# First group of a fused attention and gated-MLP kernel: products on GpSimd, scores one place ahead, no selecting products

## The chip, the cores and the metric

The kernel runs on one core of a Trainium2 chip. The metric is the device time of one execution in microseconds. Lower is better. One execution was also recorded by the hardware profiler; its span, and every instant below, counts from the span's start.

## The reference, cut to what matters

Two batches of 768 tokens with 8 heads of 48 pass a linear attention with a decaying state, then a layer with a squared relu and a sigmoid gate, then a gated layer that mixes tokens.

```python
for t in range(S):                       # attention, per batch and head
    cur = einsum('bhd,bhe->bhde', u * k_t, v_t)
    y[:, :, t] = einsum('bhd,bhde->bhe', r_t, state + cur)
    state = w_t[..., None] * state + einsum('bhd,bhe->bhde', k_t, v_t)
x = y laid out as (B, S, 384)
xk = mu_k * x + (1 - mu_k) * x_prev      # x_prev: one token back
xr = mu_r * x + (1 - mu_r) * x_prev
x = sigmoid(xr @ w_r) * (relu(xk @ w_k)**2 @ w_v)
h = gelu(x @ w_in); u, v = halves of h
v_s = einsum('ts,bsd->btd', w_sg, layernorm(v) * g) + b
out = x + (u * v_s) @ w_out
```

## The kernel before, in words

The tokens are cut into four groups of 384 (three chunks of 128), and the heads into four pairs. A unit is one pair of heads in one group, so units 0 to 3 are the first group and unit 4 opens the second. Inside a chunk the decays are turned into running products, so that the attention becomes products on TensorE (PE). The steps of unit i are these.

- Prep, on VectorE (DVE): a forward scan of the decays (`pf`), three reciprocals, a backward scan (`pr`), then `kp` = k times `pr`, `rp` = r times `pf`, and `ru` = r times k. `pr` has one buffer, `ru` two.
- S: PE transposes `kp` (`kt_ps`, which ScalarE, ACT, copies to `kt`), makes the scores `sc` from `kp` and `rp`, and sums `ru` with a small matrix `hmu` (the "sums"). DVE masks the scores (`am`, two instructions) and scales v by the sums (`vb`).
- K: PE makes each chunk's contribution to the state, `kv`; DVE chains them (`zt`, `zcar`), ACT scales them to the matrices `sblk` (and `scar`, carried to the next group).
- Y: PE applies `am` and `vb` to give `y`. Z: PE adds `sblk` times `rp`; ACT copies `y` out to `yo`, and SyncE (SP) moves its rows by DMA into `xx`, where features lie on partitions, three tiles of 128.

Then the first layer starts: `xkh` mixes a token with the one before it (ACT makes `dx`, DVE adds), one third of the features at a time, here xkh(0) to xkh(2), and PE multiplies it with eight tiles of weights, k0 to k7, three products each. Each weight tile comes by DMA as 64-bit words; ACT converts one part (`top`) and DVE joins the rest to `wk`.

The first group's order on DVE and ACT is the order in which the code is written: a class `in_order` chains these instructions. PE follows its program order everywhere. Of the rest, a scheduler orders by due times that come from a written plan (`TS`, `TE`), and instructions traced later may be placed among those of the chain. So every engine's order is fixed before the run, and an instruction that waits holds back all behind it on its engine. In the head PE also runs idle products (`dummy`).

Before the change the plan of the first group is S, K, Y, Z per unit, with the last two interleaved. GpSimd (POOL) makes only `ru`, and does so while DVE masks. Unit 1's last feature rows and those of units 2 and 3 reach xkh(1) and xkh(2) not by the DMAs but by four selecting products on PE (`sel_run`, line 650), which write them into a bank of PSUM (`sel_bank`).

Of the kernel before, what the change touches and what calls it, by code (L numbers as in the profile page):

```python
# [48 lines left out]
T_GAP = 2.5  # L49
# [14 lines left out]
ST0 = 1.04  # L64
# [6 lines left out]
def emit(tc, tin, nin, vt, consts, ucp, pars, b_sg, w_k, w_v, w_r, w_in, w_sgT, w_out, outT):  # L71
# [54 lines left out]
    u = [unit_plan(i) for i in range(NP)]  # L126
    for i in range(NP - 2):
        plan += list(u[i])
    plan += u[NP - 2][:3] + u[NP - 1][:1] + u[NP - 2][3:] + u[NP - 1][1:]
    plan = [(key, d * ST0) for key, d in plan]  # L130
# [155 lines left out]
    def load64(full, src, dl, lc=L_CV):  # L286
# [9 lines left out]
        if n_ < N_EARLY + B_STG + KF // 2:  # L296
            ld = T_EARLY + n_ * D_EARLY
# [113 lines left out]
    def attn_prep(i):  # L411
# [32 lines left out]
    def rk_make(i, e=V):  # L444
        rks[i] = pa.tile([PR, subs[i // NP][2] * CH], F32, name="ru", tag="ru", bufs=2)
        with at(TS["S", i] - L_PREP + (2 if i == 0 else -4)):
            return e.tensor_tensor(rks[i], urk[i][:, 0], urk[i][:, 1], ALU.mult).ins  # L447

    def attn_sc(i):
        tS, tK, tY = TS["S", i], TS["K", i], TS["Y", i]  # L450
# [17 lines left out]
        am = pa.tile([128, 2, nc_, CH], F32, name="am", tag="am", bufs=B_AM)
# [16 lines left out]
        if i < NP:  # L485
            sums(head["bs"][0][:, 0:2 * nc_])
        self_am(i, am, sc, tY)
        vb = pa.tile([128, nc_, 2, D], F32, name="vb", tag="vb", bufs=2)
        with at(tK - 1.6 if i >= NP else tY - 1.4):
            bh = s["bs"].rearrange("p (c h) -> p c h", h=2)[:, :, :, None].to_broadcast([128, nc_, 2, D])  # L490
            V.tensor_tensor(vb, uv[i].rearrange("p c (h d) -> p c h d", h=2), bh, ALU.mult)
        s["vb"] = vb
# [7 lines left out]
    def self_am(i, am, sc, tY):  # L500
# [75 lines left out]
    def attn_z(i):  # L576
# [58 lines left out]
    def sel_make():  # L635
        t = klpair(F32)
        sel = [t[0:PR, q * 128:q * 128 + 128] for q in range(4)]
        PL.memset(t, 0.0)
        head["sel"] = sel
        for q, rows_, to, fr in ((0, slice(32, D), 0, 32), (0, slice(HP, PR), 16, HP), (1, slice(0, D), 64, 0),  # L640
                                 (1, slice(HP, HP + 16), 112, HP), (2, slice(HP, PR), 0, HP + 16),
                                 (3, slice(0, D), 32, 0), (3, slice(HP, PR), 80, HP)):
            n = min(rows_.stop, PR) - rows_.start if q != 2 else 32
            A.activation(sel[q][rows_, to:to + n], ident[rows_, fr:fr + n], AF.Copy)

    def sel_bank(j):
        return head["bs"][j % 2]

    def sel_run(q):
        PE.matmul(sel_bank(1 + q // 2)[:, 1:1 + G], head["sel"][q], st[1 + (q + 1) // 2]["yo"], start=(q % 2 == 0), stop=(q % 2 == 1))  # L650

    def moe1_prep(s, which, hold=(), mix=None):
# [259 lines left out]
    fns = {"S": attn_sc, "K": attn_kv, "Y": attn_y, "Z": attn_z, "k": moe1_k, "r": moe1_r, "v": moe1_v,  # L912
# [39 lines left out]
    with at(TS["k", 0, 0] - 14):  # L952
        SP.dma_start(par, pars)
# [35 lines left out]
    V.memset(head["bs"][1][:, 0:1], 0.0)
    scans(0)  # L990
    products(0)
    scans(1)
# [161 lines left out]
```

## Time and profile before

| what | value |
|---|---|
| median of three runs | 340.63 us (339.87 to 341.85) |
| the profiled execution's own time | 340.49 us |
| its span | 338.6 us |
| PE busy | 329.6 us, 97% of the span |
| DVE, ACT, POOL busy | 235.9, 186.2 and 37.4 us |
| chain that ended last, PE's share | 84% |

The profiled execution takes 1.89 us more than its span, which lies around the recorded work, and stands 0.14 us under the median. PE's busy time says how long it had an instruction in flight. It counts idle products too, so the head's waits must be read from the order of instructions.

### The profile page before, as it was taken

The numbers are of one execution on the slowest core, as the hardware profiler recorded it, in microseconds if no ns is written. First come the engines' busy times: TensorE is split into PE (matmuls) and PEld (weight loads), VectorE is DVE, ScalarE is ACT, GpSimd is POOL, SyncE is SP. The second block draws the span as 40 slices with busy tenths as digits, with TensorE's granted clock in tenths as the row PEclk, the third lists the DMA queues.
The fourth block names the chain that finished last, engine by engine and source line by source line (L and its number), as shares of the span: only waits on it lengthen the run. The fifth ranks groups of instructions, "written<-read, shape, count | busy, mean of one in ns | idle before, by whom it ended". The sixth has DMA issues, their size and how long they took to land.

```text
span 338.6 us, 5946 instructions
## 1 busy us (share of the span) xinstructions
PE 329.6 (97%) x2139; PEld 286.8 (85%) x2139; DVE 235.9 (70%) x527; ACT 186.2 (55%) x444; POOL 37.4 (11%) x60
## 2 busy tenths in 40 slices
PE   7999999999999999999999999999999999999993
PEld 3785666666788899888899999989999999999993
DVE  5988987699799873996459551696889833645531
ACT  3557976568868633976339973866353216211100
POOL 3221203010110100111022531000000000000000
PEclk9999999999999999999999999999999999999998
DMA  8887955753616430011025314613230010100022
GB/s 211 211 256 256 293 190 145 195 138 99 183 58 187 115 89 9 18 38 36 19 64 180 102 57 141 171 42 82 62 81 22 1 70 2 46 25 0 0 75 77
DMA packets 24006, 34.27 MB, mean 101 GB/s; under 512 B 3568, under 2 KB 18288, under 8 KB 23968
## 3 DMA queue, kind: packets, MB, share of 16 engines
q1 hardware_dynamic: 21824, 31.39, 31.9%
q10 hardware_dynamic: 2144, 2.41, 2.9%
q8 instruction: 19, 0.31, 0.4%
q14 instruction: 19, 0.16, 0.2%
HBM read 29.07 MB, written 2.36 MB: 93 GB/s over the span
## 4 chain that ended last, share of the span: by engine, by line
PE 84%; DVE 5%; ACT 4%; DMA 3%; issue 1%; SPq 0%; ACTq 0%; DVEq 0%
PE mm L631 40%; PE mn L631 28%; PE y L570 3%; PE sc L477 3%; PE y L584 2%; DMA cst<-consts 2%; PE kv L526 1%; PE ab L473 1%; PE y L573 1%; PE kt_ps L455 1%; DMA stg<-w_in 1%; PE mm L650 1%; ACT wh L317 1%; DVE pf L425 1%; PE mm L460 1%
## 5 line engine op out<-in xcount | busy, mean ns | idle before, releaser
L619 ACT ACTIVATE gah<-gt 128x384 fp32r<-128x384 f32 x16 | 8.4, 526 | 43.4 <-DVE gt L810 43.4
L447 POOL TENSOR_TENSOR ru<-urk 112x384 f32<-112x384 f32 x15 | 17.6, 1173 | 113.3 <-DVE ru L480 81.7
L552 ACT ACTIVATE sblk<-zt,pf 48x48 f32<-48x48 f32 x62 | 20.5, 331 | 16.8 <-DVE zt L536 10.5
L716 DVE TENSOR_TENSOR kl<-kr,kh 128x384 fp32r<-128x384 f32 x24 | 15.6, 649 | 9.6 <-ACT kr L715 9.6
L631 PE MATMUL mm<-kh,wh 128*128 128x384 f32 x64 | 22.2, 347 | 0.0
L631 PE MATMUL mm<-kh,wvl 128*128 128x384 f32 x64 | 21.6, 337 | 0.0
L631 PE MATMUL mm<-kl,wh 128*128 128x384 f32 x64 | 21.5, 336 | 0.0
L631 PE MATMUL mm<-xkh,wh 128*128 128x384 f32 x57 | 20.3, 356 | 0.0
L631 PE MATMUL mn<-wsh,vl 128*128 128x384 f32 x60 | 20.0, 334 | 0.0
L631 PE MATMUL mn<-wsh,vh 128*128 128x384 f32 x60 | 20.0, 334 | 0.0
L631 PE MATMUL mn<-wsl,vh 128*128 128x384 f32 x60 | 20.0, 334 | 0.0
L665 ACT ACTIVATE dx<-xx,par 128x384 f32<-128x384 f32 x22 | 12.9, 609 | 11.6 <-DMA xx<-yo 11.5
L631 PE MATMUL mm<-xkl,wh 128*128 128x384 f32 x57 | 19.2, 338 | 0.0
L631 PE MATMUL mm<-xkh,wkl 128*128 128x384 f32 x57 | 19.2, 337 | 0.0
L506 DVE TENSOR_TENSOR am<-sc,cst 128x384 f32<-128x384 f32 x32 | 16.3, 547 | 1.9 <-PE sc L477 1.9
L477 PEld LDWEIGHTS sc<-rp,kp 48*128 48x128 f32 x192 | 12.0, 187 | 6.2 <-issue 5.6
L425 DVE TENSOR_TENSOR_SCAN pf<-uw,d1f 112x387 f32<-112x387 f32 x16 | 15.3, 957 | 2.5 <-DMA uw<-tin 2.5
L631 PE MATMUL mm<-xkh,wk 128*128 128x384 f32 x48 | 17.0, 497 | 0.0
L701 ACT ACTIVATE kr<-mm 128x384 f32<-128x384 f32 x27 | 12.9, 478 | 7.5 <-PE mm L631 7.3
L318 POOL TENSOR_TENSOR w2l<-wf,w2h 128x384 fp32r<-128x384 f32 x12 | 12.9, 1092 | 35.7 <-ACT w2h L317 35.7
L631 PE MATMUL mm<-kh,wv 128*128 128x384 f32 x48 | 16.3, 490 | 0.0
L430 DVE TENSOR_TENSOR_SCAN pr<-uw,d1r 112x387 f32<-112x387 f32 x16 | 15.8, 984 | 0.4
(218 smaller groups left out, 969.0 us busy)
## 6 DMA issues: line engine op xcount, KB each, us to landing
urk<-tin SPq DMA_DIRECT2D x26, 144.0 KB, 3.0
wh<-w_k SPq DMA_DIRECT2D x8, 384.0 KB, 4.9
stg<-w_in SPq DMA_DIRECT2D x8, 384.0 KB, 3.6
wq<-tin SPq DMA_DIRECT2D x16, 168.0 KB, 2.5
wsf<-w_sgT SPq DMA_DIRECT2D x12, 192.0 KB, 3.8
outT<-ot SPq DMA_DIRECT2D x12, 192.0 KB, 1.9
uv<-nin ACTq DMA_DIRECT2D x14, 144.0 KB, 3.5
uw<-tin SPq DMA_DIRECT2D x26, 72.8 KB, 2.9
```

The lines of the kernel that those rows point to most:

```text
L318: e.tensor_tensor(lo, full, hi.bitcast(F32), ALU.subtract)
L425: V.tensor_tensor_scan(pf[:, 0:n1], w[:, 0:n1], d1f[:, 0:n1], 1.0, ALU.mult, ALU.max)
L430: V.tensor_tensor_scan(pr[:, 1:wl][:, ::-1], w[:, 1:wl][:, ::-1], dr[:, 1:wl][:, ::-1], 0.0, ALU.mult, ALU.add)
L447: return e.tensor_tensor(rks[i], urk[i][:, 0], urk[i][:, 1], ALU.mult).ins
L477: PE.matmul(sc[h][:, c], s["kp"][hs, c], s["rp"][hs, c], start=True, stop=True)
L506: s["am"] = V.tensor_tensor(am[:, h], sc[h], mask, ALU.mult).ins
L552: s["sa"] = A.activation(sb[hs, hs], o[hs], AF.Copy, scale=s["pe"][c][hs]).ins
L570: PE.matmul(y3[hs, c], uv[i][:, c, h * D:PW if h else HP], s["at"][:, h, c], start=(c == 0), stop=False, skip_group_check=True)
L631: PE.matmul(ps, l, r, start=(first and k == 0), stop=(last and k == len(prods) - 1))
L665: ins = [A.activation(d, xj[:, 1 + t0:1 + t1], AF.Copy, scale=mu[:, j:j + 1]).ins]
L701: m1[s, "ev", f] = A.activation(kr, ps, AF.Relu).ins
L716: V.tensor_tensor(kl, kr, kh.bitcast(F32), ALU.subtract)
```

## The change

GpSimd makes `kp`, `rp` and `ru` of units 1 to 3, and `ru` of unit 0; DVE keeps unit 0's `kp` and `rp`. `hmu` is one DVE instruction instead of four on ACT. Prep runs two units ahead. S is split into T (transposes), S (scores) and U (sums), and PE takes T(i), Y(i-1), S(i), Z(i-1), U(i), K(i). The selecting products and their matrices go; xkh(1) and xkh(2) read `xx`, as xkh(0) did. Tiles k0 to k2 are done side by side, all on xkh(0), then on xkh(1), then on xkh(2). Six k weight tiles are loaded early. There are fewer idle products (two after the first scores, one before T(1)).

```diff
@@ plan
-    plan += u[NP - 2][:3] + u[NP - 1][:1] + u[NP - 2][3:] + u[NP - 1][1:]
+    for i in range(NP):
+        n = subs[0][2]
+        plan += [(("T", i), 0.13 * n)]
+        if i:
+            plan += [(("Y", i - 1), Y_D * n)]
+        plan += [(("S", i), 0.3 * n)]
+        if i:
+            plan += [(("Z", i - 1), 0.18 * n)]
+        plan += [(("U", i), 0.25 * n), (("K", i), 0.17 * n)]
@@ load64
-            ld = T_EARLY + n_ * D_EARLY
+            ld = TS["T", 1] + 0.1 * n_ if n_ < N_HEAD else TS["k", 0, 0] + (n_ - N_HEAD) * D_EARLY
@@ attn_prep
+        if 1 <= i < NP:
+            in_turn(PL.tensor_tensor, kp, k3, pr3[:, :, 0:CH], ALU.mult)
+            in_turn(PL.tensor_tensor, rp, r3, pf3[:, :, 0:CH], ALU.mult)
+            rk_make(i)
+        else:
...
+            if i == 0:
+                rk_make(0, last)
+                V.tensor_tensor(hmu, hm[:, None, :].to_broadcast([PR, NP, 2]),
+                                u_sb[:, :, None].to_broadcast([PR, NP, 2]), ALU.mult)
@@ moe1_prep
-            xj = sel_bank(j) if s == 0 and mix is not None and j else x[:, j]
+            xj = x[:, j]
@@ moe1_k
-        mm(ps, [(part(wt["k", f], slice(None), j), part(m1[s, 0], slice(None), j)) for j in range(KM)])
+        first = 3 if s == 0 and split_ops[0] else 1
+        if 0 < f < first:
+            return
+        fs = range(f, f + first if f == 0 else f + 1)
+        ps = [mm_tile()[:, 0:nt] for _ in fs]
+        for j in range(KM):
+            for p, f in zip(ps, fs):
+                mm(p, [(part(wt["k", f], slice(None), j), part(m1[s, 0], slice(None), j))], j == 0, j == KM - 1)
@@ the loop over the plan
+        if kd == "K" and g < NP - 2:
+            scans(g + 2)
+            products(g + 2)
+        if kd == "T" and 0 < g or key == ("K", NP - 1):
+            for f in st[g - 1 if kd == "T" else g].pop("soon"):
+                f()
+        if key == ("T", NP - 1):
+            conv_moe1(0, 2)
+        if key == ("Z", NP - 2):
+            mix = []
+            moe1_prep(0, 0, mix=mix)
+            mix[0]()
```

GpSimd's program in the first group, of before: four products, one per unit from unit 1 on (the last row but one belongs to unit 4), with the mixing parameters' complement `par1` among them.

```order
L447 TENSOR_TENSOR ru_207<-urk1_109 112x384
L447 TENSOR_TENSOR ru_286<-urk2_110 112x384
L447 TENSOR_TENSOR ru_365<-urk0_108 112x384
L954 TENSOR_SCALAR par1_76<-par_75 128x6
L447 TENSOR_TENSOR ru_426<-urk1_109 112x384
L611 COPY xx1_78<-xx0_77 128x3
```

The same place of the change:

```order
L463 TENSOR_TENSOR ru_159<-urk0_108 112x384
L463 TENSOR_TENSOR kp_169<-urk1_109,pr_167 112x384
L463 TENSOR_TENSOR rp_168<-urk1_109,pf_166 112x384
L463 TENSOR_TENSOR ru_175<-urk1_109 112x384
L984 TENSOR_SCALAR par1_76<-par_75 128x6
L463 TENSOR_TENSOR kp_221<-urk2_110,pr_219 112x384
L463 TENSOR_TENSOR rp_220<-urk2_110,pf_218 112x384
L463 TENSOR_TENSOR ru_227<-urk2_110 112x384
L463 TENSOR_TENSOR kp_299<-urk0_108,pr_297 112x384
L463 TENSOR_TENSOR rp_298<-urk0_108,pf_296 112x384
L463 TENSOR_TENSOR ru_305<-urk0_108 112x384
L470 TENSOR_TENSOR ru_411<-urk1_109 112x384
```

Ten products stand where three stood, in turn, `kp`, `rp`, `ru` of each unit.

DVE from the last unit's `sblk` to xkh(2), of before (`xkh` from `mm` reads a bank that a selecting product wrote; the `wk` here is k1; `pf` and `pr` are unit 4's).

```order
L550 TENSOR_SCALAR sblk11_89<-zt_445,pf_313 48x48 x2
L667 SCALAR_TENSOR_TENSOR xkh_392<-xx0_77,par1_76,dx_454 128x384
L667 SCALAR_TENSOR_TENSOR xkh_392<-mm_136,par1_76,dx_457 128x384
L425 SCALAR_TENSOR_TENSOR pf_487<-uw1_106,d1f_72 112x387
L427 RECIPROCAL d1r_90<-pf_487 112x3
L313 SCALAR_TENSOR_TENSOR wk_494<-wh_495,top1_129 128x384
L667 SCALAR_TENSOR_TENSOR xkh_392<-mm_135,par1_76,dx_500 128x384
```

The same place of the change (the five `wk` are k2 to k6):

```order
L590 TENSOR_SCALAR sblk11_89<-zt_436,pf_296 48x48 x2
L321 SCALAR_TENSOR_TENSOR wk_471<-wh_472,top0_128 128x384
L686 SCALAR_TENSOR_TENSOR xkh_420<-xx0_77,par1_76,dx_476 128x384
L321 SCALAR_TENSOR_TENSOR wk_479<-wh_480,top1_129 128x384
L433 SCALAR_TENSOR_TENSOR pf_484<-uw1_106,d1f_72 112x387
L321 SCALAR_TENSOR_TENSOR wk_576<-wh_577,top0_128 128x384
L435 RECIPROCAL d1r_90<-pf_484 112x3
L321 SCALAR_TENSOR_TENSOR wk_581<-wh_582,top1_129 128x384
L438 SCALAR_TENSOR_TENSOR pr_485<-uw1_106,d1r_90 112x387
L321 SCALAR_TENSOR_TENSOR wk_586<-wh_587,top0_128 128x384
L686 SCALAR_TENSOR_TENSOR xkh_420<-xx0_77,par1_76,dx_491 128x384
```

Nine instructions now stand between the start of k2's `wk` and xkh(2), with unit 4's two scans among them; xkh(0) has moved ahead of this piece.

ACT in the change, from the last transposes' copy to xkh(2)'s `dx` (`top0` and `top1` alternate through k0 to k6; the DMA issues of v are left out).

```order
L492 ACTIVATE kt_371<-kt_ps_367 128x336
L592 ACTIVATE sblk00_86<-zt_363,pf_218 48x48 x2
L592 ACTIVATE sblk01_87<-zt_363,pf_218 48x48 x2
L319 ACTIVATE top0_128<-wh_378 128x384
L319 ACTIVATE top1_129<-wh_383 128x384
L632 ACTIVATE yo_415<-y_387 112x384
L684 ACTIVATE dx_421<-xx0_77,par_75 128x384
L592 ACTIVATE sblk10_88<-zt_436,pf_296 48x48 x2
L632 ACTIVATE yo_459<-y_444 112x384
L319 ACTIVATE top0_128<-wh_472 128x384
L684 ACTIVATE dx_476<-xx0_77,par_75 128x384
```

The conversions of k0 and k1 stand behind unit 2's `sblk`, and that of k2 behind unit 3's `yo`.

## Rows read from the trace of the kernel before

**Rows 1.** Busy time by stretch; behind POOL: granted TensorE clock, DMA share, GB/s.
```profile
13.24:18.25 5.01, 5.01 (x64) 4.07 (x64) 4.87 (x12) 3.02 (x9) 1.00 (x1) 1.00 0.54 132
```

**Rows 2.** Timeline of DVE in the head: start us, us, instruction.
```profile
6.99 0.55 DVE L437 TENSOR_TENSOR rp<-urk,pf 112x384 f32<-112x384 f32 x1
7.46 0.55 DVE L447 TENSOR_TENSOR ru<-urk 112x384 f32<-112x384 f32 x1
7.93 0.96 DVE L425 TENSOR_TENSOR_SCAN pf<-uw,d1f 112x387 f32<-112x387 f32 x1
...
9.13 0.96 DVE L430 TENSOR_TENSOR_SCAN pr<-uw,d1r 112x387 f32<-112x387 f32 x1
10.01 1.00 DVE L506 TENSOR_TENSOR am<-sc,cst 128x384 f32<-128x384 f32 x2
10.93 0.45 DVE L491 TENSOR_TENSOR vb<-uv,mm 128x288 f32<-128x288 f32 x1
11.29 0.20 DVE L536 COPY zt<-kv 112x48 f32<-112x48 f32 x1
...
12.00 0.55 DVE L434 TENSOR_TENSOR kp<-urk,pr 112x384 f32<-112x384 f32 x1
```

**Rows 3.** Timeline of PE in unit 1 (mm from ru: the sums).
```profile
13.35 0.45 PE L455 MATMUL kt_ps<-cst,kp 112*128 112x112 f32 x3
13.73 0.94 PE L477 MATMUL sc<-rp,kp 48*128 48x128 f32 x12
14.60 0.83 PE L460 MATMUL mm<-hmu,ru 112*128 112x2 f32 x6
15.36 0.55 PE L526 MATMUL kv<-uv,kt 128*64 128x48 f32 x12
...
16.38 0.87 PE L570 MATMUL y<-am,uv 128*64 128x128 f32 x12
...
17.84 0.69 PE L584 MATMUL y<-rp,sblk 112*112 112x128 f32 x4
...
18.36 0.45 PE L455 MATMUL kt_ps<-cst,kp 112*128 112x112 f32 x3
```

**Rows 4.** Timelines where POOL and DVE work at once, alone at 15.64.
```profile
15.64 1.00 POOL L447 TENSOR_TENSOR ru<-urk 112x384 f32<-112x384 f32 x1 [4.00 <-DVE am L506]
...
52.62 1.76 POOL L447 TENSOR_TENSOR ru<-urk 112x384 f32<-112x384 f32 x1 [10.40 <-DVE wv L313]
...
53.87 1.33 DVE L430 TENSOR_TENSOR_SCAN pr<-uw,d1r 112x387 f32<-112x387 f32 x1
...
57.59 0.96 DVE L425 TENSOR_TENSOR_SCAN pf<-uw,d1f 112x387 f32<-112x387 f32 x1
57.75 1.59 POOL L447 TENSOR_TENSOR ru<-urk 112x384 f32<-112x384 f32 x1 [3.37 <-DVE ru L480]
```

**Rows 5.** Timeline from 22 to 46 us, several engines: start us, us, instruction.
```profile
29.42 0.49 ACT L596 ACTIVATE yo<-y 112x384 f32<-112x384 f32 x1 [0.97 <-PE y L584]
...
32.20 2.23 PEld L631 LDWEIGHTS mm<-xkh,wk 128*128 128x128 f32 x8 [0.65 <-DVE xkh L667]
...
34.89 0.45 PE L455 MATMUL kt_ps<-cst,kp 112*128 112x112 f32 x3
...
36.72 4.14 PE L631 MATMUL mm<-xkh,wk 128*128 128x384 f32 x12
36.82 1.12 ACT L311 ACTIVATE top<-wh 128x384 f16<-128x384 bf16 x2
...
37.86 1.02 DVE L313 SCALAR_TENSOR_TENSOR wk<-wh,top 128x384 uint32<-128x384 uint32 x2
```

**Rows 6.** Instructions on sblk up to 40 us (duration ns min/median/max).
```profile
L552 ACT ACTIVATE sblk<-zt,pf x14: 329/332/336, 11.5 to 27.0; 48x48 f32<-48x48 f32 x14
```

**Rows 7.** What is on xx up to 50 us: its transfers, issue to landing.
```profile
DMA to landing us min/median/max: 2.0/3.3/3.9
```

**Rows 8.** DMA issues of v weights in line: xcount, KB each, median us to landing.
```profile
kl<-w_v SPq DMA_DIRECT2D x4, 384.0 KB, 7.0
```

More of the change, by code (lines that the diff above doesn't have):

```diff
@@ L48 @@
 UPIN = 11
-T_GAP = 2.5
+T_GAP = 0.2
 T_TAIL = 9.0
@@ new lines, in attn_prep, with in_turn, rk_make @@
+        st[i] = dict(rp=rp, kp=kp, pe=[pf3[:, c, CH:CH + 1] for c in range(nc_)])
+    rks = {}
+    def in_turn(f, *a):
+        with contextlib.ExitStack() as c:
+            if "pool" in head:
+                c.enter_context(tc.issue_after(head["pool"]))
+            head["pool"] = f(*a).ins
+        return head["pool"]
+    def rk_make(i, beside=None):
+        rks[i] = pa.tile([PR, subs[i // NP][2] * CH], F32, name="ru", tag="ru", bufs=2)
+        with at(TS["S", i] - L_PREP - (4 if i >= NP else 0)):
+            a = (PL.tensor_tensor, rks[i], urk[i][:, 0], urk[i][:, 1], ALU.mult)
+            ins = in_turn(*a) if i < NP else a[0](*a[1:]).ins
+        if beside is None:
+            return
+        tc.add_manual_dep(ins, beside.name, mybir.DependencyInfo(
+            mybir.DependencyClass.Sync, mybir.DependencyReason.DATA), reason="beside other work of VectorE")
@@ L451, in attn_sc, with sums, attn_t @@
+    def sums(i, bs):
+        nc_ = subs[i // NP][2]
+        st[i]["bs"] = bs
+        for c in range(nc_):
+            PE.matmul(bs[:, 2 * c:2 * c + 2], rks[i][:, c * CH:(c + 1) * CH], hmu[:, i % NP], start=True, stop=True)
+    def attn_t(i):
         s = st[i]
@@ L484, in attn_sc @@
             return
-        if i < NP:
-            sums(head["bs"][0][:, 0:2 * nc_])
         self_am(i, am, sc, tY)
[L488 to L492, printed above, removed]
+        if i >= NP:
+            rows_by_sums(i)
     def hbu(i):
@@ L508, in self_am @@
         s["at"] = am
-        if i + 1 < NU:
-            tc.add_manual_dep(rk_make(i + 1, PL), s["am0"].name, mybir.DependencyInfo(
-                mybir.DependencyClass.Sync, mybir.DependencyReason.DATA), reason="beside the masks")
+        if NP <= i + 1 < NU:
+            rk_make(i + 1, s["am0"])
     def attn_kv(i):
@@ L633, in emit @@
     m1 = {}
[L635 to L650, printed above, removed]
     def moe1_prep(s, which, hold=(), mix=None):
@@ L951, in emit @@
     load_n(1)
-    with at(TS["k", 0, 0] - 14):
+    with at(TS["T", 1] + 0.06):
         SP.dma_start(par, pars)
@@ L981, in emit @@
     manual.__enter__()
-    head["ps"], head["bs"] = mm_tile(), [mm_tile(), mm_tile()]
+    head["ps"], head["bs"] = mm_tile(), mm_tile()
     dummy(ND0)
-    for j in range(NP):
-        A.activation(hmu[:, j], hm, AF.Copy, scale=u_sb[:, j:j + 1])
-    sel_make()
     head["order"] = in_order()
     head["order"].__enter__()
[L989 to L992, printed above, removed]
+    for i in range(2):
+        scans(i)
+        products(i)
     keys = [key for key, _ in plan if key]
```

111 lines of the change are left out of this document (49 added, 62 removed).

## The prediction

> **What bounds the kernel now.** I read the busy time by stretch first, then the timelines of the engines in the head, then those of the first layer. In the stretch of unit 1 [rows 1] DVE is busy 4.87 of 5.01 us; PE reads 5.01 too, but that counts idle products and instructions in flight. The granted TensorE clock is 1.00 there, the 2.4 GHz level, so nothing here is about the clock. PE goes from T(1) at 13.35 to T(2) at 18.36, 5.01 us [rows 3]. DVE's own loop has that length. From start to start it is scans 1.20 (`pf` to `pr`, 7.93 to 9.13), 0.88 to the masks, 0.92 to `vb`, 0.36 to `zt`, 0.71 to `kp` [rows 2], and `kp` and `rp`, each worth the 0.47 from `rp` to `ru` in the same rows: 5.01. So in the head DVE is the bound, and 0.94 of a unit is what the change takes from it. Later, PE waits 0.65 for xkh(2) at 32.20, then runs on: T, U, S of unit 4 from 34.89, k2 and k3 from 36.72 to 40.86 [rows 5]. PE then goes on without a longer wait to 40.86 and beyond, so I compare the two kernels by the end of k3: what it comes earlier or later by, the end does.
>
> **The head, step by step.** `ru` of unit 0 leaves DVE (0.47), and `hmu` comes to it, 112 x 8; I take 0.07 (it lies between nothing and `ru`'s 0.47; eight columns of 384 are near the lower end). So `pf`(1) runs from 7.53 instead of 7.93, to 8.49. But the new `ru` on POOL waits for `rp`'s end at 7.54 and meets that scan. What such a meeting costs the rows of before show [rows 4]. `ru` on POOL takes 1.00 alone, beside masks. When a scan was running (57.59 to 58.55) it ended at 59.34, 0.79 after the scan. When POOL was first (to 54.38), DVE's `pr` took 1.33 and ended 0.82 after POOL. So two SBUF-reading instructions of the pair run one after the other, with some 0.2 of overlap. The masks, `vb` and `zt` read PSUM, and the row at 15.64 lies beside masks at its full speed.
>
> With that, POOL's `ru`(0) ends at 8.49 + 0.79 = 9.28, `pr`(1) at 9.28 + 0.82 = 10.10, and the masks of unit 0 start 0.08 before that end, at 10.02. Before it was 10.01: the head start is eaten.
>
> Then each unit goes round this loop: `pr` ends, `kp` on POOL (0.07 for the handover, 1.00, beside masks), `rp` (1.00, beside `vb` and `zt`), `pf` of the next unit ends 0.82 after it, `ru` 0.79 after that, `pr` 0.82 after that. The sum is 4.50, against 5.01. DVE reaches `pf` in time: the masks start 0.08 before `pr` ends, and 0.92 + 0.36 + 0.71 later, 1.91 after that end, is before `rp`'s end at 2.07. PE's own work per unit is no lower: 0.38 + 0.87 + 0.76 from T to K, 0.55 for K, 1.46 from Y to Z and 0.52 from Z to T [rows 3], 4.54. The new order of PE puts 1.46 or more between every product and what it waits for on ACT, so I cost those handovers at nothing; without that cover a `kt` or `sblk` would cost its 0.33 to 0.5.
>
> In the Trainium skill the page "SBUF — State Buffer", section "Who interferes with whom", says that a DVE instruction with two SBUF inputs and a GpSimd instruction that reads SBUF block each other, the second until the first finishes. The rows agree on the order but give 0.79 and 0.82 where the page's full stop would give 1.00 and 0.96; by the page the loop is 4.99, and the sum below would be about a microsecond later.
>
> So `pr`(2) ends at 14.60. `par1` stands ahead of `kp`(2) on POOL, and I add 0.2 (nothing to 1.00; six columns of 384). `pr`(3) ends at 14.60 + 0.2 + 4.50 = 19.3, `kp`(3) at 20.37, T(3) runs 20.4 to 20.85.
>
> **The last unit.** Here ACT's order decides. `kt`(3) takes about 0.45 (`yo`, slightly wider, takes 0.49 [rows 5]), four `sblk` 4 x 0.33 [rows 6], to 22.7; only then come the `top`s of k0 and k1, 1.12 for two [rows 5], to 23.8. DVE's `wk` of k1 follows (1.02 for two), and the masks of unit 3 stand behind it: 24.4, though their scores are there at about 23.2. From there DVE needs 0.92, xkh(0) 0.55 (like a `wk`, a little more), `vb` 0.36, `zt` 0.71, two small `sblk` 0.5: 27.4. Z(3) ends at 27.9 and `yo`(3) at 28.4, 1.5 before the 29.91 of before.
>
> **The first layer.** The selecting products go, which were PE's and hid nothing else. What the DMA route costs is landing: 2.0 to 3.9 [rows 7] after an issue at 28.5 to 29.0, so xx is whole at 31 to 33. This is hidden if PE has work, and it has: six products on xkh(0) and xkh(1), 4.1 by the row at 36.72. But DVE does not come to xkh(2) then. ACT's `top` of k2 stands behind `yo`(3), so k2's `wk` starts at 28.4 + 0.64 + 0.05 = 29.1, and nine instructions lie from its start to xkh(2): five `wk` at 0.51, xkh(1) 0.55, two scans and the reciprocals, 1.85 since other work fills the gap between them (2.08 by rows 2 without that). 29.1 + 4.95 = 34.05, and xkh(2) ends at 34.65. ACT's `dx`(2), behind the `top` of k6, which waits for the buffer that k4's `wk` frees at about 32.1, runs at 32.7, so it is not what is late.
>
> PE: k0 and k1 on xkh(0) from 27.75 to 29.1, k2 after its `wk` at 29.7, xkh(1)'s three until 32.45, then a wait of 2.25. The last three run 34.7 to 36.75, T, U, S of unit 4 take 1.83 (34.89 to 36.72), k3 half of the 4.14: 40.65, against 40.86. The gain is 0.2. The 1.5 us that the head gives are paid back by conversions that stand ahead of xkh(2); from `yo`(3)'s end to the third slice it is 2.3 then (29.91 to 32.20) and 6.3 now, and the three tiles side by side fill 2.8 of the difference with four more products.
>
> Moved DMAs: k2 to k5 are issued before the transfers of `yo`(0) on SP, 1.5 MB in front of them, but xkh(0) wants those rows only at 24.3, some four microseconds after `yo`(1). Behind k3 I see no step that gains: the conversions that come early ran beside a busy PE before. Against the profiled execution, 340.49 - 0.2 = **340.3 us**. That execution stands 0.14 under the median, which I leave out of the sum.
>
> **The rivals.**
>
> *The transfer is really hidden.* If k3 to k6 are joined outside the chain to xkh(2), because ACT and DVE get to them before `yo`(3) ends or faster than the rows say, xkh(2) follows the landing: 31.0 + 0.6 + 0.6 = 32.2, before PE is done at 32.45. Then the 2.25 go: 338.1. For it: PE has the work, and the shorter landings. Against it: the order on both engines.
>
> *POOL and DVE don't meet.* If `kp` and `rp` delay no scan, the head keeps the 0.40 of `pf`(1)'s earlier start, the loop falls to PE's 4.54, `par1` costs nothing: about 0.6 earlier, 339.7. The rows at 52.62 and 57.75 speak against it.
>
> *They stop each other whole.* Loop 0.07 + 1.00 + 1.00 + 0.96 + 1.00 + 0.96 = 4.99, twice 0.49 later: 341.3. Against it are the 0.79 and 0.82. It is also about what it costs if POOL's next product is served before a waiting scan.
>
> *The last rows land late (slower).* The transfer of `yo`(3) is issued right behind the load of k6 and ahead of five more weights. Weights issued in line took 7.0 to land [rows 8]. At that price xx is whole at 36.05, `dx` and xkh(2) end at 37.3, and PE starts 2.65 later: 342.9. It decides from a landing after 33.4, when `dx`(2) would end behind DVE's 34.05. Against it: 3.9 is the longest that xx took.
>
> **How the numbers follow.** Chances: forecast 0.46, hidden 0.22, not meeting 0.08, whole stop 0.08, late rows 0.16. The likeliest case's own range is 339.2 to 341.6: below, a step of 0.5 less on DVE and 0.6 of the head; above, the loop at 4.99 and 0.3 of small waits. If in addition k4 to k6 run `top` and `wk` one after the other, 3 x 0.62 come on top, 342.2. The range 338.0 to 342.2 takes in the hidden transfer, and leaves out most of the late rows. A measurement of this kernel can tell about 0.5%, 1.7 us, from no change. Faster than that: hidden 0.22 and 0.06 from the forecast's and the not-meeting case's lower ends, 0.28. Slower: late rows 0.14 (0.02 land between) and 0.03 of the others' upper ends, 0.17. No change: 0.55.
>
> **What would show it.** Masks start about 4.5 apart in units 0 to 2, POOL's products beside scans take well over 1.00, and masks of unit 3 stand behind k1's `wk`. PE should wait about 2 us ahead of the third slice of k0, for xkh(2) on DVE, with xx landed by then. If PE has no such wait, the hidden case holds. If the wait is longer and ACT's `dx`(2) waits for DMA, the late rows do. If the loop is 5.0 or 4.4 I have mis-sized the meeting. I am wrong altogether if PE loses or gains over a microsecond behind k3.

## The result, and the profile after

| | before | changed |
|---|---|---|
| median | 340.36 us | 345.29 us (344.78 to 346.45, four runs) |
| ratio | | 1.0142, 95% interval 1.0099 to 1.0186 |
| profiled execution's time and span | 340.49, 338.6 us | 345.75, 343.7 us |
| masks of units 0 to 3 start | 10.01, 15.03, 20.04, 24.56 | 9.72, 14.69, 19.65, 24.95 |
| k3 of the first group ends | 40.86 | 42.2 |
| T(7), T(8) start on PE | 66.96, 88.24 | 68.48, 92.85 |

The change is 4.9 us slower, 1.4%. I had forecast 340.3 (338.0 to 342.2). From the span's start to T(7) it loses 1.5 us, from T(7) to T(8) 3.1, and behind that 0.5.

The page of the changed kernel, engines' busy time and the shares of the chain that ended last:

```profile
PE 327.4 (95%) x2130; PEld 285.3 (83%) x2130; DVE 236.1 (69%) x519; ACT 183.7 (53%) x433; POOL 43.4 (13%) x66
...
PE 71%; ACT 7%; DVE 6%; DMA 3%; issue 2%; SPq 0%; ACTq 0%; DVEq 0%
```

PE's busy time is 2.2 us lower, and its share of the chain falls from 84% to 71%: PE waits for others now. The places follow in order of time.

GpSimd (POOL) and VectorE (DVE) in the head, timelines of the changed kernel, the answer to [rows 2, 4]:

```profile
9.88 0.96 POOL L463 TENSOR_TENSOR kp<-urk,pr 112x384 f32<-112x384 f32 x1 [0.90 <-DVE pr L438]
10.78 0.92 POOL L463 TENSOR_TENSOR rp<-urk,pf 112x384 f32<-112x384 f32 x1
11.65 1.02 POOL L463 TENSOR_TENSOR ru<-urk 112x384 f32<-112x384 f32 x1
...
14.85 0.95 POOL L463 TENSOR_TENSOR kp<-urk,pr 112x384 f32<-112x384 f32 x1 [1.36 <-DVE pr L438]
...
30.34 1.15 POOL L470 TENSOR_TENSOR ru<-urk 112x384 f32<-112x384 f32 x1 [7.75 <-DMA uv<-nin]
```

```profile
9.72 0.99 DVE L547 TENSOR_TENSOR am<-sc,cst 128x384 f32<-128x384 f32 x2
...
11.70 1.79 DVE L433 TENSOR_TENSOR_SCAN pf<-uw,d1f 112x387 f32<-112x387 f32 x1
...
13.80 0.96 DVE L438 TENSOR_TENSOR_SCAN pr<-uw,d1r 112x387 f32<-112x387 f32 x1
14.69 0.99 DVE L547 TENSOR_TENSOR am<-sc,cst 128x384 f32<-128x384 f32 x2
```

The forward scan `pf` comes at 11.70, just as `rp` ends. But POOL has begun `ru` at 11.65, so the scan takes 1.79 and ends 0.82 after `ru`. Then the reciprocals and `pr` run alone. The loop is 4.96.

DVE in the first layer (the second row is xkh(1), the last xkh(2); `wk` are k2, then k3 to k6):

```profile
30.07 0.56 DVE L321 SCALAR_TENSOR_TENSOR wk<-wh,top 128x384 uint32<-128x384 uint32 x1 [2.08 <-ACT top L319]
30.55 1.36 DVE L686 SCALAR_TENSOR_TENSOR xkh<-xx,par,dx 128x384 f32<-128x384 f32 x1
...
32.30 0.95 DVE L433 TENSOR_TENSOR_SCAN pf<-uw,d1f 112x387 f32<-112x387 f32 x1
...
34.16 0.95 DVE L438 TENSOR_TENSOR_SCAN pr<-uw,d1r 112x387 f32<-112x387 f32 x1
35.03 0.52 DVE L321 SCALAR_TENSOR_TENSOR wk<-wh,top 128x384 uint32<-128x384 uint32 x1
35.48 0.60 DVE L686 SCALAR_TENSOR_TENSOR xkh<-xx,par,dx 128x384 f32<-128x384 f32 x1
```

xkh(2) stands where the order put it, behind the conversions and both scans. xkh(1) meets POOL's `ru` of unit 4 (30.34 to 31.49) and takes 1.36 instead of 0.61.

PE of the changed kernel, the instructions that waited, with T(3) and T(8), the answer to [rows 3, 5]:

```profile
20.82 0.51 PE L487 MATMUL kt_ps<-cst,kp 112*128 112x112 f32 x3 [0.47 <-POOL kp L463]
...
36.14 2.20 PE L667 MATMUL mm<-xkh,wk 128*128 128x384 f32 x6 [1.97 <-DVE xkh L686]
...
74.04 1.32 PE L610 MATMUL y<-am,uv 128*64 128x128 f32 x12 [0.45 <-DVE am L547]
...
89.91 0.44 PE L667 MATMUL mm<-xkh,wh 128*128 128x384 f32 x1 [1.03 <-ACT xkh L689]
90.82 0.45 PE L667 MATMUL mm<-xkl,wh 128*128 128x384 f32 x1 [0.47 <-DVE xkl L690]
...
92.85 0.35 PE L487 MATMUL kt_ps<-cst,kp 112*128 112x112 f32 x2
```

The three waits from 74 on did not exist before. They lie 30 us and more behind the first layer's first tiles, the last stage that the change touches. What stands ahead of them is DVE's order. Before, from unit 8's forward scan (timeline of DVE):

```profile
66.86 0.96 DVE L425 TENSOR_TENSOR_SCAN pf<-uw,d1f 112x387 f32<-112x387 f32 x1
67.73 0.53 DVE L594 TENSOR_TENSOR yo<-y,ru 112x384 f32<-112x384 f32 x1
...
68.39 0.96 DVE L430 TENSOR_TENSOR_SCAN pr<-uw,d1r 112x387 f32<-112x387 f32 x1
...
70.18 1.01 DVE L506 TENSOR_TENSOR am<-sc,cst 128x384 f32<-128x384 f32 x2
71.11 0.55 DVE L437 TENSOR_TENSOR rp<-urk,pf 112x384 f32<-112x384 f32 x1
```

And in the changed kernel:

```profile
68.70 0.95 DVE L433 TENSOR_TENSOR_SCAN pf<-uw,d1f 112x387 f32<-112x387 f32 x1
...
69.91 0.96 DVE L438 TENSOR_TENSOR_SCAN pr<-uw,d1r 112x387 f32<-112x387 f32 x1
70.79 0.53 DVE L630 TENSOR_TENSOR yo<-y,ru 112x384 f32<-112x384 f32 x1
...
72.17 1.35 DVE L450 TENSOR_TENSOR rp<-urk,pf 112x384 f32<-112x384 f32 x1
73.44 1.01 DVE L547 TENSOR_TENSOR am<-sc,cst 128x384 f32<-128x384 f32 x2
```

`yo` of unit 6 has fallen behind unit 8's `pr`. Unit 7's masks, which stood between unit 8's `kp` and `rp`, now stand behind both, and `rp` meets POOL besides. From `pf`'s start the masks come 3.3 us later before, 4.7 now. The `yo` of unit 7 moves in the same way behind unit 10's `pr`, from 78.97 (that `pr` came at 83.23) to 83.56:

```profile
82.68 0.96 DVE L438 TENSOR_TENSOR_SCAN pr<-uw,d1r 112x387 f32<-112x387 f32 x1
83.56 0.53 DVE L630 TENSOR_TENSOR yo<-y,ru 112x384 f32<-112x384 f32 x1
```

Its rows go to xkh(2) of the second group, for which PE waits at 89.91.

The span's 5.1 us then are: 1.5 up to T(7), 1.1 at unit 7's masks (75.29 against 72.66 for the products behind Y(7), less the 1.5), 2.0 from there to T(8), of which the two waits are 1.5, and 0.5 later.

### The profile page after: what moved, and what is told of

Same layout as the page of the kernel before. It is cut to its first block, busy times and chain, and to the rows that moved or that the text cites. A ratio compares the mean times of both kernels' runs of the same rounds, so it can differ in the third digit from the quotient of the medians.

```text
span 343.7 us, 5917 instructions
## 1 busy us (share of the span) xinstructions
PE 327.4 (95%) x2130; PEld 285.3 (83%) x2130; DVE 236.1 (69%) x519; ACT 183.7 (53%) x433; POOL 43.4 (13%) x66
## 4 chain that ended last, share of the span: by engine, by line
PE 71%; ACT 7%; DVE 6%; DMA 3%; issue 2%; SPq 0%; ACTq 0%; DVEq 0%
PE mm L667 36%; PE mn L667 26%; ACT wh L325 2%; PE y L610 2%; PE sc L523 2%; DMA stg<-w_in 2%; PE y L624 1%; DMA stg<-w_v 1%; DVE pf L433 1%; PE ab L519 1%; ACT top L319 1%; PE kv L566 1%; DVE am L547 1%; ACT sblk L592 1%; PE kt_ps L487 1%
## 5 line engine op out<-in xcount | busy, mean ns | idle before, releaser
L470 POOL TENSOR_TENSOR ru<-urk 112x384 f32<-112x384 f32 x12 | 13.6, 1137 | 112.8 <-DVE ru L526 89.1
L667 PE MATMUL mm<-kh,wh 128*128 128x384 f32 x72 | 24.7, 344 | 0.0
L667 PE MATMUL mm<-kh,wvl 128*128 128x384 f32 x72 | 24.2, 336 | 0.0
L667 PE MATMUL mm<-kl,wh 128*128 128x384 f32 x72 | 24.2, 336 | 0.0
L684 ACT ACTIVATE dx<-xx,par 128x384 f32<-128x384 f32 x24 | 14.1, 609 | 13.1 <-DMA xx<-yo 12.9
L433 DVE TENSOR_TENSOR_SCAN pf<-uw,d1f 112x387 f32<-112x387 f32 x16 | 16.9, 1058 | 2.3 <-DMA uw<-tin 2.3
L610 PE MATMUL y<-am,uv 128*48 128x128 f32 (+1 forms) x192 | 15.9, 278 | 1.9 <-DVE am L547 1.7
L667 PEld LDWEIGHTS mm<-xkh,wk 128*128 128x128 f32 x48 | 8.5, 189 | 9.6 <-DVE xkh L686 3.5
```

The source lines that it names most:

```text
L433: V.tensor_tensor_scan(pf[:, 0:n1], w[:, 0:n1], d1f[:, 0:n1], 1.0, ALU.mult, ALU.max)
L470: ins = in_turn(*a) if i < NP else a[0](*a[1:]).ins
L610: PE.matmul(y3[hs, c], uv[i][:, c, h * D:PW if h else HP], s["at"][:, h, c], start=(c == 0), stop=False, skip_group_check=True)
L667: PE.matmul(ps, l, r, start=(first and k == 0), stop=(last and k == len(prods) - 1))
L684: ins = [A.activation(d, xj[:, 1 + t0:1 + t1], AF.Copy, scale=mu[:, j:j + 1]).ins]
```

## The experiments

The theory: the loss has two roots that don't depend on each other. One is in the head and the first layer, where POOL and xkh(2) are waited for. The other is the order on DVE around units 6 to 10, which is set anew by the scheduler because the three k tiles stand side by side. The rival: nothing is wrong with the order, everything is just late and short of time. All ratios are to the kernel before, run beside each version on the same chip (its medians there: 340.34 to 340.57). T(7) and T(8) are from PE's timelines, of one profiled execution each.

| run | median us | ratio, 95% interval | T(7) | T(8) | between |
|---|---|---|---|---|---|
| before | | | 66.96 | 88.24 | 21.28 |
| changed | 345.29 | 1.0142 (1.0099 to 1.0186) | 68.48 | 92.85 | 24.37 |
| c_order | 341.82 | 1.0030 (1.0015 to 1.0045) | 68.76 | 90.30 | 21.54 |
| k_alone | 345.22 | 1.0130 (1.0100 to 1.0160) | 68.14 | 91.75 | 23.61 |
| k_alone_order | 342.78 | 1.0068 (1.0046 to 1.0090) | 69.54 | 90.75 | 21.21 |
| k_one | 345.72 | 1.0151 (1.0137 to 1.0166) | 72.47 | 93.70 | 21.23 |
| x2_first | 343.90 | 1.0088 (1.0067 to 1.0109) | 66.53 | 92.76 | 26.23 |
| ru_dve | 344.66 | 1.0106 (1.0075 to 1.0137) | 69.55 | 93.17 | 23.62 |
| ru_behind_pf | 345.80 | 1.0148 (1.0127 to 1.0169) | 70.06 | 94.27 | 24.21 |
| meet_clean | 344.43 | 1.0112 (1.0094 to 1.0130) | 67.78 | 93.33 | 25.55 |
| x2_order | 341.27 | 1.0017 (0.9996 to 1.0038) | 67.17 | 88.91 | 21.74 |
| k2_order | 340.14 | 1.0019 (0.9980 to 1.0059) | 66.26 | 88.31 | 22.05 |
| all_four | 340.74 | 1.0012 (0.9988 to 1.0036) | 67.58 | 88.81 | 21.23 |
| all_five | 341.04 | 1.0019 (1.0002 to 1.0036) | 66.20 | 88.28 | 22.08 |

### The order behind the first group: c_order, k_alone, k_alone_order, k_one

c_order puts three edges into the changed kernel, on DVE only. An edge makes one instruction wait for another: unit 8's `pr` for unit 6's `yo`, unit 8's products for unit 7's masks, and unit 9's `pr` for unit 7's `yo` (`ev` is unit g's `yo`; the first `next` traces the forward scan, the second the backward one):

```diff
+        if kd == "S" and g == 7:
+            with tc.issue_after(st[7]["am"]):
+                products(8)
+        if kd == "Z" and g in (6, 7):
+            load_unit(g + 3)
+            head["prep", g + 2] = attn_prep(g + 2)
+            next(head["prep", g + 2])
+            with tc.issue_after(st[g]["ev"]):
+                next(head["prep", g + 2])
+            if g == 7:
+                products(9)
```

> The changed kernel with three edges on VectorE around the first group's last units: the backward scan of unit 8 behind the yo of unit 6, the products of unit 8 behind the masks of unit 7, the backward scan of unit 9 behind the yo of unit 7 (about the order of the kernel before there). Nothing of the computation changes. Theory 'order': of the 5.1 us of span lost, 1.5 stand at T(7) and come from ahead of it, and 3.1 to 3.5 come between 69 and 93 us from VectorE's new order there. With the old order the masks of unit 7 start about 1 us earlier, the wait of PE at k of group 1 (1.0 for xkh, 0.5 for xkl) goes, and the time is 342.0 (341.5 to 342.8). Rival 'carried': VectorE and ScalarE are short of time there because everything starts 1.5 us later, the order is not the cause, and the time stays at 344.5 or more.

341.82, as the theory of the order says. DVE of c_order at the same place:

```profile
69.80 0.53 DVE L630 TENSOR_TENSOR yo<-y,ru 112x384 f32<-112x384 f32 x1
70.25 0.95 DVE L438 TENSOR_TENSOR_SCAN pr<-uw,d1r 112x387 f32<-112x387 f32 x1
...
71.56 1.01 DVE L547 TENSOR_TENSOR am<-sc,cst 128x384 f32<-128x384 f32 x2
72.49 0.65 DVE L447 TENSOR_TENSOR kp<-urk,pr 112x384 f32<-112x384 f32 x1
```

T(7) is no earlier than in the changed kernel, and yet T(8) is 2.6 earlier. The three waits are gone. So three edges, which change no work, give back 3.5 of 4.9 us. In the profiled executions 2.8 us of this lie between T(7) and T(8). The edges don't restore the order of before exactly: there unit 8's `kp` stood ahead of the masks, and unit 9's `pr` ahead of unit 7's `yo`. They were not tried one by one.

k_alone takes moe1_k's three k tiles side by side into the kernel before, and nothing else:

```diff
+        first = 3 if s == 0 and split_ops[0] else 1
+        if 0 < f < first:
+            return
+        fs = range(f, f + first if f == 0 else f + 1)
```

> The kernel before with one part of the change alone: the first three k tiles of group 0 side by side, slice by slice. Theory 'order': it moves yo of unit 6 and the masks of unit 7 on VectorE behind the scans and products of unit 8, as in the changed kernel, though nothing in the head is changed; it saves most of the 0.65 us wait for the third slice and loses about 3 us behind 69 us: 342.8 (341.8 to 343.5). Rival: the late order costs only where PE is already late, and the kernel is at 339.7 to 340.5.

345.22, worse than I expected (341.8 to 343.5): by the medians this part alone costs as much as the whole change. The profiled execution took 343.76, 3.3 more than before, of which 1.2 stand at T(7) and 2.3 between T(7) and T(8). DVE and then PE of k_alone:

```profile
68.99 0.96 DVE L430 TENSOR_TENSOR_SCAN pr<-uw,d1r 112x387 f32<-112x387 f32 x1
69.88 0.53 DVE L594 TENSOR_TENSOR yo<-y,ru 112x384 f32<-112x384 f32 x1
...
73.40 0.99 DVE L506 TENSOR_TENSOR am<-sc,cst 128x384 f32<-128x384 f32 x2
```

```profile
33.91 4.78 PE L631 MATMUL mm<-xkh,wk 128*128 128x384 f32 x14 [1.96 <-DVE wk L313]
```

`yo` of unit 6 is behind unit 8's `pr` and the masks are late again, without anything changed in the head. In the first layer PE now wants k2's weight earlier than its conversion comes, and waits 1.96. k_alone_order adds the three edges to it.

> k_alone with the three edges of c_order on VectorE: the kernel before, its k tiles of group 0 side by side, and the old order around units 6 and 7. k_alone lost 1.4 at T(5), where PE waits 1.96 for the conversion of k2 that it now needs earlier, and 2.3 between T(7) and T(8). Theory: the second loss goes, the first stays: 342.9 (342.0 to 343.6). Rival: the order follows from being late and the edges only move the wait, 344.5 or more.

342.78: the second loss goes, the first stays. The time between T(7) and T(8) is 21.21 again. That T(7) is 1.4 later than in k_alone was there at T(1) already (14.54 against 13.13): the granted clock of this execution was 0.52 and 0.62 between 10 and 14 us.

k_one is the changed kernel with `first = 1`, no edge added.

> The changed kernel with one part undone: the k tiles of group 0 one after the other again, not three side by side. By the order in which VectorE's program stands, yo of unit 6 then comes ahead of the backward scan of unit 8 again and the masks of unit 7 ahead of its products, with no edge of mine. Theory 'order': PE's wait for xkh(2) now comes with one tile in front of it, 2.8 longer, so T(5) stands near 49.9 (2.7 after the changed kernel, less 0 to 1 where conversions catch up), but the 3 us behind 69 us are not lost: 344.0 (343.0 to 345.0). Rival 'carried': the loss behind 69 us comes from everything being late, grows with it, and the time is 346.5 or more.

The time, 345.72, lies between the two theories, so the median alone decides nothing. The table says more: PE is 4 us later at T(7) than in the changed kernel, and still takes only 21.23 to T(8). So being late doesn't cause the loss, and the rival falls. But the theory fails here too in one part. I expected the old order without the side-by-side tiles, and DVE of k_one does not have it:

```profile
69.05 0.96 DVE L433 TENSOR_TENSOR_SCAN pf<-uw,d1f 112x387 f32<-112x387 f32 x1
...
70.26 0.96 DVE L438 TENSOR_TENSOR_SCAN pr<-uw,d1r 112x387 f32<-112x387 f32 x1
...
71.74 0.55 DVE L450 TENSOR_TENSOR rp<-urk,pf 112x384 f32<-112x384 f32 x1
...
73.08 0.53 DVE L630 TENSOR_TENSOR yo<-y,ru 112x384 f32<-112x384 f32 x1
...
74.95 1.00 DVE L547 TENSOR_TENSOR am<-sc,cst 128x384 f32<-128x384 f32 x2
```

As in the changed kernel, unit 8's two scans stand ahead of unit 6's `yo`, its products ahead of unit 7's masks, and unit 10's `pr` (81.82) ahead of unit 7's `yo` (83.62). Yet this costs nothing here. DVE has done unit 8's scans and products before PE reaches T(7), at 72.47: unit 8's `pf` starts 3.4 ahead of T(7), in the changed kernel 0.2 behind it. The masks come 2.5 behind T(7), against 5.0 in the changed kernel and 3.2 before, and unit 7's `yo` 11.2, against 15.1 and 12.0. I read this so: the swapped order costs only where PE comes early enough to wait for it. The tiles side by side are enough to bring the order (k_alone) but not needed for it (k_one).

What I also missed is a cost in the first layer: PE waits 2.50 for xkh(1) and 3.26 for xkh(2), and behind the first of these waits its clock falls to half. A window of k_one (PE busy, weight loads, DVE, ACT, POOL, then granted clock, DMA share, GB/s):

```profile
34.00:36.00 2.00, 0.00 (x0) 0.00 (x0) 2.00 (x4) 1.98 (x7) 0.00 (x0) 0.50 0.95 310
```

In the six kernels that have the tiles side by side and none of the three edges (changed, k_alone, x2_first and the three of the head) T(7) to T(8) takes 23.6 to 26.2. The two longest, x2_first and meet_clean, lost some of that to a granted clock of 0.50 ahead of T(8); the other four lie between 23.6 and 24.4 at full clock. In the eight others it is 21.2 to 22.1. Why the scheduler's plan gives the new order is not shown. It is not `T_GAP`, a constant of the plan that the change also sets from 2.5 to 0.2: with 2.5 the changed program has the same order on DVE there (read from the program, not run), and k_alone has 2.5.

### The head: ru_dve, ru_behind_pf, meet_clean

ru_dve makes `ru` of units 1 to 3 on DVE, between the two scans:

```diff
             V.reciprocal(pe, pf3[:, :, CH:CH + 1])
+        if 1 <= i < NP:
+            rk_dve(i)
         yield
...
-            rk_make(i)
...
+    def rk_dve(i):
+        rks[i] = pa.tile([PR, subs[i // NP][2] * CH], F32, name="ru", tag="ru", bufs=2)
+        V.tensor_tensor(rks[i], urk[i][:, 0], urk[i][:, 1], ALU.mult)
```

> The changed kernel with the product ru of units 1 to 3 back on VectorE, between its two scans; kp and rp stay on GpSimd. Theory 'meeting': the loop of a unit was 4.96 because GpSimd's ru starts just ahead of the next forward scan and holds it; without it the loop is 0.07 + 0.88 + 0.90 for kp and rp, 0.82 more for the scan, 0.1, 0.47 for ru and 0.88, 4.1 in all, under PE's 4.54: masks 4.5 to 4.6 apart, T(3) at 19.7 to 20.0 instead of 20.82. What follows in the first layer waits for the same conversions, so of this 0.9 at most 0.5 stands at the end: 344.7 to 345.4. Rival: PE's own row or the masks set the loop and it stays at 4.9.

The masks come 4.41 and 4.45 apart, and no scan is stretched:

```profile
12.24 0.96 DVE L433 TENSOR_TENSOR_SCAN pf<-uw,d1f 112x387 f32<-112x387 f32 x1
...
13.79 0.96 DVE L440 TENSOR_TENSOR_SCAN pr<-uw,d1r 112x387 f32<-112x387 f32 x1
14.66 1.00 DVE L552 TENSOR_TENSOR am<-sc,cst 128x384 f32<-128x384 f32 x2
```

T(3) is 0.5 earlier, 20.35 (I expected 19.7 to 20.0), but T(4) 0.9 later, 39.12. Behind the wait for xkh(2) (1.98, as in the changed kernel) the clock fell in this execution (window of ru_dve, columns as above):

```profile
37.00:38.00 1.00, 1.00 (x3) 0.49 (x2) 0.29 (x2) 1.00 (x3) 0.00 (x0) 0.50 1.11 338
```

ru_behind_pf keeps `ru` on POOL and lets that of units 1 and 2 wait for the next unit's forward scan (`s_`).

```diff
+            if 2 <= i < NP:
+                rk_make(i - 1, s_.ins)
```

> The changed kernel in which GpSimd's ru of units 1 and 2 waits for the forward scan of the next unit, which my prediction took for granted. Theory 'who comes first': the scan then runs ahead of ru, and the loop is 0.07 + 0.88 + 0.90 for kp and rp, 0.82 for the scan, 1.0 for ru beside the reciprocals, 0.82 for the backward scan: 4.5, masks 4.5 apart, T(3) 0.8 to 0.9 earlier. Rival 'stop each other whole': 4.95 as in the changed kernel. At the end 0.3 to 0.8 earlier at most: 344.5 to 345.3.

It failed as an experiment. `par1` stood between `rp` and `ru`, waited there for its transfer until 13.35, and `ru` and the next `kp` with it; the masks came 4.14 and then 6.82 apart. meet_clean is the same with `par1` at the end of POOL's head.

```diff
-    PL.tensor_scalar(par1, par[:, 0:2 * KM], -1.0, 1.0, ALU.mult, ALU.add)
...
             products(g + 2)
+            if g == NP - 3:
+                in_turn(PL.tensor_scalar, par1, par[:, 0:2 * KM], -1.0, 1.0, ALU.mult, ALU.add)
```

> ru_behind_pf again, with par1 (which waited for its transfer between rp and ru of unit 1 there) at the end of GpSimd's head. Theory 'who comes first': VectorE reaches the forward scan 1.91 after the backward one ended, just as rp ends, so the scan runs unhindered for 0.95; ru behind it takes 0.07 and 0.95 to 1.0, and the backward scan ends 0.82 after ru: 4.7 to 4.8 a unit (4.5 if ru and scan overlap as they do without the wait), against 4.96. Rival 'stop each other whole': 4.95 to 5.0. T(3) 0.4 to 0.9 earlier; at the end 344.7 to 345.6.

The loops are 4.76 and 4.85, and T(3) is 0.3 earlier than in the changed kernel. POOL's `ru`, then DVE's scans of meet_clean:

```profile
12.78 1.00 POOL L466 TENSOR_TENSOR ru<-urk 112x384 f32<-112x384 f32 x1 [1.04 <-DVE pf L433]
```

```profile
11.75 0.95 DVE L433 TENSOR_TENSOR_SCAN pf<-uw,d1f 112x387 f32<-112x387 f32 x1
...
13.02 1.58 DVE L440 TENSOR_TENSOR_SCAN pr<-uw,d1r 112x387 f32<-112x387 f32 x1
```

With the scan first, `pr` ends 0.82 after `ru` (14.60 against 13.78), in the second unit 0.82 too. So the size of the meeting in the prediction holds, and who comes first is worth 0.1 to 0.2 us a loop here. The 4.50 of the prediction is not reached: the edge makes `ru` wait for the scan's end, so the two don't overlap.

### The first layer, and versions put together: x2_first, x2_order, k2_order, all_four, all_five

x2_first moves xkh(2) between the scans of unit 4 and holds the later conversions back:

```diff
             next(rest)
+            head["mix2"] = mix[2]()
             next(rest)
-            mix[2]()
...
-            conv_moe1(4)
+            with tc.issue_after(head["mix2"][0]), tc.issue_after(head["mix2"][1]):
+                conv_moe1(4)
```

> The changed kernel with xkh(2) of group 0 between the two scans of unit 4, and the conversions of k4 and later behind it on ScalarE and VectorE. Theory: xkh(2) then follows the landing of the last rows (about 32.5 to 33.0) and starts at 33.2 instead of 35.48; PE's wait ahead of the third slice falls from 2.0 to about 0.2 and k3 ends 1.7 to 2.0 earlier, near 40.3. The order behind 50 us is that of the changed kernel, so the end follows by 1 to 2: 343.3 to 344.5. Rival 'late rows': the wait stays, on a transfer, and the time is 345.0 or more. Rival 'moved wait': PE waits for kp of unit 4 instead and gains at most 0.5.

xkh(2) starts at 33.71, PE's wait ahead of the third slice goes (one of 1.51 for k2's weight comes at 31.77), and T(7) is at 66.53, 0.4 ahead of the kernel before. Then it takes 26.2 to T(8), with the masks of unit 7 waited for 1.52 at 73.16 and the clock down behind the wait for the second group's xkh(2). The median is 343.90. x2_order has c_order's edges as well.

> x2_first and c_order together: xkh(2) between the scans of unit 4 with the later conversions behind it, and the three edges around units 6 and 7. x2_first had T(7) at 66.53, 0.4 ahead of the kernel before, and lost it to T(8) (26.2 between them); c_order took 21.5 there. Theory: T(8) near 88.1, the time 339.8 (339.0 to 340.6), the level of the kernel before. Rival 'gain of x2_first is lost behind anyway': 341.5 or more.

341.27: 1.5 over the forecast. T(8) is at 88.91 instead of 88.1. PE waits 1.32 for k2's weight at 31.56, and 1.07 for unit 4's `sblk` at 45.56, where its two parts waited 0.22 and 0.41. k2_order takes ACT's `top` of k2 ahead of unit 3's `sblk`, and DVE's half behind them (load64 puts that half into the list `later`).

```diff
+        if key == ("K", NP - 1):
+            head["later"] = []
+            conv_moe1(2, 3)
+            later = head.pop("later")
...
+        if key == ("K", NP - 1):
+            for f in later:
+                f()
```

> x2_order, and ScalarE's top of k2 ahead of the small sblk of unit 3 (ScalarE idles 2 us there), with VectorE's half of the conversion right behind the sblk. In x2_first PE waited 1.5 for that weight at 30.2 to 31.8, and VectorE idled from 28.1 to 30.2. Theory: the wait goes; PE reaches the third slice at about 33 instead of 34 and then waits there for xkh(2), whose rows land at 32.5 and which ends at 33.6 to 34.3: 0.4 to 1.0 less than x2_order, 339.1 (338.3 to 340.0). Rival: everything waits for the landing and nothing is gained on x2_order.

340.14 (339.65 to 343.90), above the 339.1 that I expected. Its ratio, 1.0019, is no lower than x2_order's 1.0017, so no gain on x2_order is shown. The wait for the weight is gone, and PE reaches the third slice at 33.2 and waits 0.89 there:

```profile
34.11 2.20 PE L673 MATMUL mm<-xkh,wk 128*128 128x384 f32 x6 [0.89 <-DVE xkh L692]
```

all_four adds ru_dve, and holds unit 10's backward scan behind the second group's xkl(2).

```diff
+        if kd == "Z" and g == 8:
+            load_unit(11)
+            head["prep", 10] = attn_prep(10)
+            next(head["prep", 10])
+            with tc.issue_after(head["x1"][1]):
+                next(head["prep", 10])
+                products(10)
```

> k2_order with ru of units 1 to 3 on VectorE as in ru_dve, and the backward scan and the products of unit 10 behind xkl(2) and xrl(2) of group 1. The first takes the loop from 4.96 to 4.45, and T(3), the masks of unit 3, the landing of the last rows and the third slice come about 0.5 earlier; the second takes the 0.56 that PE waited for xkl at 86.29. Theory: 339.1 (338.3 to 340.0), the lowest so far and below the kernel before by 0.4%. Rival: the head's half microsecond is lost again, since T(4) or the weights of k3 to k6 are not ready earlier: 339.7 to 340.5.

340.74, a little above the rival's range too. Windows of all_four behind the waits at 33.22 and 44.28:

```profile
46.00:48.00 2.00, 2.00 (x13) 1.28 (x10) 2.00 (x5) 1.67 (x5) 0.00 (x0) 0.65 1.06 363
48.00:50.00 2.00, 2.00 (x4) 1.09 (x4) 2.00 (x5) 0.00 (x0) 0.81 (x1) 0.50 0.68 226
```

all_five also holds unit 5's backward scan behind unit 4's `zt`.

```diff
+        if key == ("K", NP):
+            with tc.issue_after(st[NP]["zt"]):
+                next(head["prep", NP + 1])
+            products(NP + 1)
```

> all_four, and the backward scan and the products of unit 5 on VectorE behind the zt of unit 4. In all_four the second zt of unit 4 stood behind that scan, the last sblk came at 44.2, PE waited 0.73 for it at 44.28 (1.02 for xkh(2) at 33.22 before that), and the granted clock fell to 0.50 between 46.7 and 50.0, which cost some 1.7 us between T(5) and T(6) (12.0 against 10.3 in k2_order). Theory: the wait goes and with it most of the clock's loss: 339.0 (338.4 to 339.9), below the kernel before by 0.4%. Rival: the clock falls by the first of the two waits, or elsewhere, and the time stays at 340.2 or more.

341.04, the rival again. The wait for `sblk` is gone, and one of 0.70 for unit 5's `kp` stands at 44.91 in its place. The six of its twelve executions with a mean granted clock of 0.995 or more took 339.17 to 340.75, the six with 0.990 to 0.992 took 341.32 to 342.65. No version is shown to beat the kernel before, whose clock was 0.995 or more in all 17 executions beside it. So the changed kernel can be brought back to its level, and no further by these runs.

## Why the prediction was wrong

Right, or only off in size:

- The wait for xkh(2): forecast 2.25 with the third slice at 34.7, measured 1.97 at 36.14. The reason given, conversions and unit 4's scans ahead of it, is what x2_first shows: with xkh(2) moved ahead, the wait goes.
- The masks of unit 3 stand behind k1's `wk`: forecast 24.4, measured 24.95. The last rows did not land late: in x2_first ACT takes them at 32.50. In the changed kernel ACT's `dx`(2) runs at 34.25 instead of 32.7, still ahead of what holds DVE.
- The size of a meeting of POOL and DVE, 0.82 in the changed kernel and in meet_clean.
- `hmu` held the next scan back by 0.08 (7.15 to 7.23), where I had taken 0.07, and `par1` cost nothing where I had added 0.2.

Wrong, in the order of what it cost:

- "Behind k3 I see no step that gains", and with it "what it comes earlier or later by, the end does". 3.6 of the 5.1 us of span arise behind T(7). I compared the two programs at three places of the head and the first layer, and took the rest for unchanged since its code is. But an order that a scheduler writes can change anywhere. The prediction named a loss of over a microsecond behind k3 as the sign that it is wrong altogether, and this is that case. c_order shows that the order on DVE costs some 3 us there, and k_alone that the tiles side by side are enough to bring it. What brings it without them, in k_one, stays open.
- "Nine instructions lie from its start to xkh(2)": the count was right, but xkh(1) at 0.55 was not. I let POOL and DVE meet in the head and forgot `ru` of unit 4, so xkh(1) took 1.36, 0.8 more, of which 0.5 are left at xkh(2). With that, 0.55 at unit 3's masks and 0.4 between them and `yo`, k3 ends at 42.2 where I had 40.65.
- "DVE reaches `pf` in time." I set POOL's two products at 1.00 each, from rows in which one stands alone [rows 4]. Queued behind each other they end 1.82 after `kp`'s start. `rp` ends at the instant at which the scan comes, and `ru` goes first. The loop is 4.96, not 4.50.

The 4.96 looks like my rival of a whole stop, 4.99, but it isn't one: the scan ended 0.82 after `ru`, not its full 0.96. That rival also named the case that POOL's next product goes ahead of the scan, at about the same price, and that is close to what came. With the scan first the loop is 4.8 (meet_clean), and with `ru` off POOL 4.4 (ru_dve). In the Trainium skill the page "SBUF — State Buffer", section "Who interferes with whom", says that the order of issue decides who blocks. The trace agrees: 0.05 us between POOL's `ru` and DVE's scan decided it.

Of the rivals, the hidden transfer, the engines that don't meet and the late rows did not occur.

## What to carry to other kernels

Where a scheduler writes an engine's order, compare the whole program's order before and after, not only near the edit: a few swaps far behind it, in code that nobody touched, were worth some 3 us here, and three edges gave that back. The order alone doesn't say what it costs: k_one has the swaps too and lost nothing there, with PE 4 us later. Where two engines exclude each other, ask at each meeting who comes first, down to a tenth of a microsecond, and look for meetings in every stage that the moved work reaches. A saved wait counts only up to the next thing that is late: each of the versions put together moved PE's wait to another weight, another `sblk` or another `kp`.

## What the runs showed of the hardware

- A POOL product of 112 x 384 takes 0.95 to 1.00 alone, but queued ones start 0.86 to 0.92 apart (changed kernel, 9.88 to 22.6).
- DVE's conversions, mixes and products that read two tiles of SBUF are held by POOL like the scans are: k2's `wk` took 1.39 instead of 0.56 (x2_first, 30.23), xkh(1) 1.36 instead of 0.61, `rp` 1.35 instead of 0.55 (both in the changed kernel).
- PE's granted clock fell from 1.00 to 0.50, from 2.4 to 1.2 GHz, for some 3 to 7 us behind waits of PE of 0.7 to 3.3 us (k_one, ru_dve, all_four), though not behind every such wait: the changed kernel's 1.97 at 36.14 had none.
